# Block 0's attention logits: summed over features through DRAM and VectorE instead of on TensorE

## The chip, the core and the metric

The kernel runs on one core of one Trainium2 chip. The metric is the device time of one execution in microseconds (us), the median of several runs; lower is better. A core has engines that run side by side and wait for each other by semaphores: TensorE (matrix products, called PE in the profile; PEld is its loading of weights), VectorE (DVE), ScalarE (ACT), GpSimd (POOL) and SyncE (SP), which here only issues transfers. 16 DMA engines move data between DRAM and the on-chip memory SBUF. TensorE writes to PSUM, eight banks here, from which VectorE and ScalarE read.

## The reference

Two layers alternate, each twice, on x of 2048 tokens by 1024 features in bfloat16. Every layer normalises x over its features, computes a sum to add to x, and adds it.

```python
# layer A, on the normalised x; H = 32 heads of Dh = 32, W = 8 positions at a distance of 2
qkv = (x @ wqkv).reshape(B, S, 3, H, Dh).transpose(2, 0, 3, 1, 4)
q, k, v = qkv[0], qkv[1], qkv[2]
idx = pos[:, None] - (jnp.arange(W) * 2)[None, :]
logits = jnp.einsum("bhsd,bhswd->bhsw", q, kg) * Dh ** -0.5     # kg, vg: k, v at idx
logits = jnp.where(idx >= 0, logits, -1e9)
o = jnp.einsum("bhsw,bhswd->bhsd", softmax(logits), vg)
return o.transpose(0, 2, 1, 3).reshape(B, S, D) @ wo
# layer B, on the normalised x; F = 3584
return (relu(x @ W_gate) * (x @ W_up)) @ W_down
# x = x + A(x); x = x + B(x); x = x + A(x); x = x + B(x)
```

So each token attends to itself and to seven earlier tokens, 2 to 14 positions back. A logit is the sum, over the 32 features of a head, of q times k.

## The kernel before

The tokens are cut into four blocks of 512, each block into four token tiles of 128. The four layers are numbered L = 0 to 3. TensorE's work is laid out in one sequence by hand: the q, k and v products of blocks 0 to 3 in layer 0 (`plan_proj`), with the output product of block 0 (`plan_wo`, called through `wo`) put between two groups of block 3; then for each block the gate and up products of layer 1 (`plan_gu`), an output product, and the down products (`plan_down`), and so on. A group is eight matmuls of 128x512 into one PSUM bank.

All instructions are given to a planner, `Plan`, with an estimated time. `on_pe` adds matmuls and advances a clock at 0.216 us each (`MM`). `at(t, f)` puts a step at time t. `on_dve` and `chain` hold VectorE's work: the chain is done in order, each link once its input is due, and the `on_dve` pieces go in between at their times. `slab` loads 1 MB of weights into the next free slot of a ring of five. In the end all steps are sorted by time and recorded in that order, so the times only decide the order in which the instructions stand in each engine's queue; on the chip every engine goes through its queue in order and waits where an input is missing. The plan's time 0 is some 7 to 11 us after the start of the profiled span.

Layer 0's block 0 is special (`first_logits`). For the other blocks q, k and v go through DRAM, and come back with a partition for each pair of token tile and head, where VectorE multiplies and sums over features within a partition (`mul`, `add3`, `fold` in `plan_attn`). For block 0 the columns of q and k are taken so that chunk c of eight holds, on partition p, feature 8p + c: four neighbouring partitions hold a head's 32 features, eight in each. They stay in SBUF. As each k chunk c arrives, VectorE multiplies it by q for all eight positions (`mul(c)`, 128x4096) and adds the product to two f32 sums, one for each half of the positions (`add(c, h)`, `lacc`). Chunk 7 is not added. The sums are split into bfloat16 terms: ScalarE casts (`split`), VectorE subtracts the cast (`rest`), twice, giving three terms; with the last product these are four 128x4096 operands. TensorE then sums the four partitions of each head by multiplying with the 0/1 matrix `wide` (`red`, 32 matmuls into two banks, four groups of columns each), ScalarE copies the result to SBUF (`out`), and the softmax (`soft_a`, `expo`, `soft_b`) starts. `red` stands in TensorE's sequence behind the first v group of the second half of block 1 (`step`, hooked at `("v", 1, 0)`).

After the softmax VectorE multiplies with v and sums over the positions (`pv_mul`, `pv_add`, eight pieces); each piece is stored to `o_d`, and SyncE reloads it transposed, in four pieces (`load_o`, the tile `oT`), for the output product. That is hooked behind step `("k", 0, 2)` of block 3. The output product is added to x, and `plan_ln` normalises x for layer 1; a transposing transfer of SyncE (`turn`, the tile `xnT`) brings it to the layout that the gate product needs.

In the start, SyncE issues, in this order: x of block 0, half of v's weights, q's weights, x of block 1, k's weights (into two ring slots), v's other half (`wv_0_1`), x of block 2; then the transposes of block 1's normalised x, the output weights, and x of block 3. `late_ln` normalises the blocks 1 to 3 at given times.

Of the kernel before, what the change touches and what calls it, by code (L numbers as in the profile page):

```python
# [9 lines left out]
BF16 = mybir.dt.bfloat16  # L10
# [6 lines left out]
H = 32  # L17
# [106 lines left out]
def kernel(  # L124
# [42 lines left out]
    neg_half = const.tile([P, TPB], F32, name="neg_half")  # L167
    zpad = const.tile([P, KC, HALO], BF16, name="zpad")
    maskc = const.tile([32, W, HALO], F32, name="maskc")
    wide = const.tile([P, H], BF16, name="wide")  # L170
    ring = wring.tile([P, 8 * RING, SLAB], BF16, name="ring")
    q_d = [dram.tile([D, BLK], BF16, name=f"q_d{b}") for b in range(NB)]
    k_d = [dram.tile([D, ROW], BF16, name=f"k_d{b}") for b in range(NB)]
    v_d = [dram.tile([D, ROW], BF16, name=f"v_d{b}") for b in range(NB)]
    o_d = [dram.tile([TPB, H, DH, P], BF16, name=f"o_d{b}") for b in range(NB)]
    x_blk = [xpool.tile([P, TPB, D], BF16, name=f"xb{b}") if b else None for b in range(NB)]
    x_tiles = [x_blk[t // TPB][:, t % TPB, :] if t >= TPB else xpool.tile([P, D], BF16, name=f"x{t}") for t in range(NT)]
# [5 lines left out]
        nc.gpsimd.memset(neg_half[:], -0.5)  # L183

    def consts_late():
        nc.gpsimd.memset(wide[:], 1.0)
        nc.gpsimd.affine_select(out=wide[:], in_=wide[:], pattern=[[-FG, H]], compare_op=ALU.is_ge,
                                fill=0.0, base=0, channel_multiplier=1)
        nc.gpsimd.affine_select(out=wide[:], in_=wide[:], pattern=[[FG, H]], compare_op=ALU.is_ge,
                                fill=0.0, base=FG - 1, channel_multiplier=-1)  # L190
        nc.gpsimd.memset(zpad[:], 0.0)
        for t in (v_d, k_d):
            nc.gpsimd.dma_start(_dram(t[0], 0, [[ROW, P], [P * ROW, KC], [1, HALO]]), zpad[:])
        nc.gpsimd.memset(maskc[:], 0.0)
        for w in range(1, W):
            nc.gpsimd.memset(maskc[:, w, 0:DIL * w], NEG)

    def slab(src_ap, name, start=-10.0):
        shp = list(src_ap.shape)

        def load():
            s["t"] = ring[:, 8 * s["slot"]:8 * s["slot"] + shp[1], 0:shp[2]]
            nc.sync.dma_start(s["t"], src_ap)

        s = plan.slab(load, start)
        return s
# [251 lines left out]

    def first_logits(st, tm):
        hold = {}
        terms = []

        def begin():
            hold["q"] = hm_pool.tile([P, KC, BLK], BF16, tag="q", name="q_fm")
            hold["k"] = hm_pool.tile([P, KC, HALO + BLK], BF16, tag="k", name="k_fm")
            nc.gpsimd.memset(hold["k"][:, :, 0:HALO], 0.0)

        def evict(nm, c, acc, t):
            def f():
                if nm == "q":
                    nc.scalar.copy(hold["q"][:, c, :], acc()[:])
                    return
                kt = hold["k"]
# [24 lines left out]
        def add(c, h):  # L501
            def f():
                if c == 1:
                    hold[("acc", h)] = tpose.tile([P, W // 2, BLK], F32, tag="T", name=f"lacc{h}")
                acc, ws = hold[("acc", h)], slice(4 * h, 4 * h + 4)
                nc.vector.tensor_tensor(acc[:], hold[("pr", 0)][:, ws] if c == 1 else acc[:], hold[("pr", c)][:, ws], op=ALU.add)
            return f

        def split(n, h):

            def f():
                if h == 0:
                    terms.append(at_pool.tile([P, W, BLK], BF16, tag="pr", name="term_0", bufs=2) if n == 0 else
                                 hm_pool.tile([P, W, BLK], BF16, tag="k", name="term_1"))
                nc.scalar.copy(terms[n][:, 4 * h:4 * h + 4], hold[("acc", h)][:])

            def after(now):
                t = max(now + 0.2, tm.get(("split", n, 0), 0.0))
                plan.at(t, f)
                tm[("split", n, h)] = t + 2.4  # L520
            return after

        def rest(n, h):
            def f():
                acc = hold[("acc", h)]
                if n == 1 and h == 0:
                    terms.append(hm_pool.tile([P, W, BLK], BF16, tag="q", name="term_2"))
                nc.vector.tensor_tensor(acc[:] if n == 0 else terms[2][:, 4 * h:4 * h + 4], acc[:],
                                        terms[n][:, 4 * h:4 * h + 4], op=ALU.subtract)
            return f  # L530

        def red():
            Ls = hold["L"] = [psum.tile([P, 4, P], F32, tag="acc", name=f"L{wh}") for wh in range(2)]
            for n, term in enumerate([hold[("pr", KC - 1)]] + terms):
                for wh in range(2):
                    for tq in range(TPB):
                        nc.tensor.matmul(Ls[wh][32 * tq:32 * tq + 32, :, :], lhsT=wide[:],  # L537
                                         rhs=term[:, 4 * wh:4 * wh + 4, tq * P:(tq + 1) * P],
                                         start=(n == 0), stop=(n == 3), skip_group_check=True, tile_position=(0, 32 * tq))

        def out():
            st["L"] = at_pool.tile([P, W, P], F32, tag="L", name="L_0_0")
            for wh in range(2):
                nc.scalar.copy(st["L"][:, 4 * wh:4 * wh + 4, :], hold["L"][wh][:])

        def step():
            e = plan.on_pe(9.5, red)
            plan.at(e + T_EV, out)
            tm["logits_in"] = e + T_EV + 1.5

        return {"evict": evict}, {("v", 1, 0): step}


    def plan_attn(L, b, ends, st, tm):
# [121 lines left out]
            plan.at(t + 0.2, expo)  # L676
            tm["exp"] = t + 2.2

        plan.chain.append(((lambda: tm["logits_in"]) if first else now, 3.0, soft_a, after_a))
        plan.chain.append((lambda: tm["exp"], 4.0, soft_b, None))  # L680

        def after_pv(t):
# [128 lines left out]
    wo_start = []  # L811
    attn = {}
    glu = {}
    later_hooks = []
    wo_hook = {("k", 0, 2): lambda: wo(0, 0)}

    def proj(L, b):
        st, tm = {}, {}
        if L == 0 and b == 0:
            hooks, later_hooks[:] = (lambda h: (h[0], [h[1]]))(first_logits(st, tm))  # L820
        else:
            hooks = later_hooks.pop() if later_hooks else wo_hook if L == 0 and b == NB - 1 else {}
        attn[(L, b)] = plan_attn(L, b, plan_proj(L, b, hooks), st, tm)

    def wo(L, b):
# [99 lines left out]
```

## Time and profile before

| what | value |
|---|---|
| median of 3 runs | 1621.34 us (1621.14 to 1622.3) |
| the profiled execution | 1621.7 us, its span 1620.0 us |
| TensorE busy | 1609.8 us, 99% of the span |
| VectorE, ScalarE, GpSimd busy | 1060.6, 450.5 and 111.1 us |
| granted TensorE clock, mean | 1.00 |
| q, k and v products of block 0 and 1 end at | 53.8 and 97.2 us |
| softmax of block 0 starts at | 93.04 us |
| output product of block 0 | 150.75 to 164.7 us |
| first gate product of layer 1 | 193.91 us |

The span is from the first to the last profiled instruction; the time of an execution is a little longer. A line of the timeline names start, length, engine, line of the kernel, operation, output and inputs, and how many instructions are merged (x4); in square brackets stands the idle time before it and what ended that. Matmuls overlap: a single one is shown with some 0.38 us, and they start 0.216 apart. The chain of waits is followed back from the last instruction to whatever released each step. "Landing" is the time from the issue of a transfer until its data are in place.

### The profile page before, as it was taken

The page shows a single profiled execution, that of the slowest core. Times are in us where ns is not written, and L with a number is a line of the kernel's source. Part 1 is how long each engine was busy: PE and PEld are TensorE (multiplying, and loading weights), DVE is VectorE, ACT ScalarE, POOL GpSimd, SP SyncE. Part 2 cuts the span into 40 slices and gives each one's busy share as a digit, 9 for nine tenths or more (in the row PEclk, how much of TensorE's full clock was granted, in tenths as well). Part 3 has the DMA queues.
Part 4 walks back from the last instruction along what each step waited for, and adds up shares of the span by engine and source line. Part 5 has one row for each costly group of instructions (what it writes and reads, how often), then busy time and mean ns, then how long its engine had stood idle before and what let it go on. Part 6 is the DMA issues. An engine that isn't in the chain of part 4 may idle for free.

```text
span 1620.0 us, 19174 instructions
## 1 busy us (share of the span) xinstructions
PE 1609.8 (99%) x7609; PEld 745.5 (46%) x7658; DVE 1060.6 (65%) x1284; ACT 450.5 (28%) x707; POOL 111.1 (7%) x172
## 2 busy tenths in 40 slices
PE   8999999999999999999999999999999999999999
PEld 6444444444444444444444444444444444444444
DVE  6999989989999269960699617986989212211211
ACT  4753421304131241312413251133011311221110
POOL 3221000001010100011000110000000000000000
PEclk9999999999999999999999999999999999999999
DMA  9765878868965887668876699599846655564452
GB/s 299 162 157 136 222 197 219 189 190 216 223 181 196 231 206 206 189 204 234 198 202 195 212 240 209 159 281 225 228 155 194 184 169 163 175 186 152 156 167 68
DMA packets 443755, 314.83 MB, mean 194 GB/s; under 512 B 195568, under 2 KB 437648, under 8 KB 443664
## 3 DMA queue, kind: packets, MB, share of 16 engines
q1 hardware_dynamic: 414496, 281.39, 64.7%
q10 hardware_dynamic: 24368, 23.40, 4.4%
q0 software_dynamic: 4800, 8.80, 1.6%
q8 instruction: 60, 0.98, 0.3%
q14 instruction: 31, 0.25, 0.0%
HBM read 261.77 MB, written 36.05 MB: 184 GB/s over the span
## 4 chain that ended last, share of the span: by engine, by line
PE 98%; DMA 1%; SPq 1%; issue 0%; DVE 0%; DVEq 0%
PE acc_u L736 24%; PE acc_g L736 24%; PE dacc L782 24%; PE acc_k L401 7%; PE acc_wo L706 7%; PE acc_v L401 6%; PE acc_q L401 6%; DMA ring<-in_A_wqkv_dram 1%; SPq L850 0%; PE L L537 0%; SPq L834 0%; SPq L861 0%; DVE xb L790 0%; SPq L854 0%; SPq L838 0%
## 5 line engine op out<-in xcount | busy, mean ns | idle before, releaser
L736 PEld LDWEIGHTS <-ring 128*128 128x128 bf16 x3584 | 350.7, 98 | 422.9
L736 PE MATMUL acc_g<-xnT,ring 128*128 128x512 bf16 x1792 | 423.3, 379 | 0.0
L736 PE MATMUL acc_u<-xnT,ring 128*128 128x512 bf16 x1792 | 423.3, 379 | 0.0
L782 PE MATMUL dacc<-ring,hT 128*128 128x512 bf16 (+1 forms) x1787 | 386.4, 376 | 1.7
L751 DVE TENSOR_TENSOR hT<-acc_u,r 128x512 bf16<-128x512 f32 x224 | 154.3, 689 | 322.3 <-PE acc_u L736 316.7
L743 ACT ACTIVATE r<-acc_g 128x512 bf16<-128x512 f32 x224 | 133.6, 596 | 706.4 <-PE acc_g L736 706.4
L782 PEld LDWEIGHTS <-hT 128*128 128x128 bf16 x1820 | 178.1, 98 | 209.0
L401 PEld LDWEIGHTS <-ring 128*128 128x128 bf16 x1152 | 115.5, 100 | 134.0 <-DMA ring<-in_A_wqkv_dram 1.0
L627 DVE TENSOR_TENSOR pvt<-a,vhm 128x4096 bf16<-128x4096 bf16 x64 | 146.2, 2284 | 0.2
L586 DVE TENSOR_TENSOR l<-l,pr 128x1024 f32<-128x1024 f32 x112 | 136.8, 1221 | 2.3
L576 DVE TENSOR_TENSOR pr<-qhm,khm 128x4096 bf16<-128x4096 bf16 x56 | 127.9, 2283 | 13.1 <-DMA khm<-k_d 13.1
L401 PE MATMUL acc_k<-xnT,ring 128*128 128x512 bf16 x512 | 113.5, 379 | 0.6 <-DMA ring<-in_A_wqkv_dram 0.6
L706 PE MATMUL acc_wo<-ring,oT 128*128 128x512 bf16 x496 | 111.0, 379 | 0.8
L790 DVE TENSOR_TENSOR xb<-dacc,xb 128x512 bf16<-128x512 f32 (+1 forms) x49 | 32.6, 678 | 120.4 <-PE dacc L782 120.0
L401 PE MATMUL acc_v<-xnT,ring 128*128 128x512 bf16 x384 | 84.4, 379 | 0.0
L635 DVE TENSOR_TENSOR pvt<-pvt 128x2048 bf16<-128x2048 bf16 x64 | 78.1, 1221 | 1.3
L638 POOL DMA_DIRECT2D o_d<-ohm x64 | 35.3, 552 | 623.4 <-DVE ohm L637 612.6
L706 PEld LDWEIGHTS <-oT 128*128 128x128 bf16 x512 | 50.1, 98 | 60.4
L410 ACT CAST stage_q<-acc_q 128x512 bf16<-128x512 f32 x56 | 32.2, 583 | 148.7 <-PE acc_q L401 147.8
L586 DVE TENSOR_TENSOR l<-pr 128x1024 f32<-128x1024 bf16 x56 | 68.2, 1218 | 0.6
L593 DVE TENSOR_TENSOR l<-l 128x512 f32<-128x512 f32 x112 | 62.3, 556 | 3.0
L261 POOL TENSOR_TENSOR rstd<-vpe,neg_half 128x2 f32<-128x2 f32 x26 | 26.7, 1026 | 540.8 <-DVE vpe L260 540.6
(92 smaller groups left out, 844.9 us busy)
## 6 DMA issues: line engine op xcount, KB each, us to landing
ring<-in_B_W_gate_dram SPq DMA_DIRECT2D x56, 1024.0 KB, 7.0
ring<-in_B_W_up_dram SPq DMA_DIRECT2D x56, 1024.0 KB, 5.5
ring<-in_B_W_down_dram SPq DMA_DIRECT2D x48, 1024.0 KB, 6.1
ring<-in_A_wqkv_dram SPq DMA_DIRECT2D x27, 1024.0 KB, 5.4
ring<-in_A_wo_dram SPq DMA_DIRECT2D x16, 1024.0 KB, 7.0
vhm<-v_d SPq DMA_DIRECT2D x32, 284.0 KB, 7.0
v_d<-stage_v ACTq DMA_DIRECT2D x32, 256.0 KB, 6.0
o_d<-ohm POOLq DMA_DIRECT2D x64, 128.0 KB, 3.9
```

The lines of the kernel that those rows point to most:

```text
L401: nc.tensor.matmul(acc[:, t0 * P:t1 * P], lhsT=lhsT, rhs=xnT[(L, b)][:, t0:t1, kc, :], start=(kc == 0), stop=(kc == KC - 1))
L576: nc.vector.tensor_tensor(pr[:], st["q"][:], _ap(st["k"], HALO - DIL * w, [[HALO + P, DH], [1, P]]), op=ALU.mult)
L586: nc.vector.tensor_tensor(l[:], pr[:, 0:8] if i == 0 else l[:], pr[:, 8 * i + 8:8 * i + 16], op=ALU.add)
L593: nc.vector.tensor_tensor(l[:, 0:n], l[:, 0:n], l[:, n:2 * n], op=ALU.add)
L627: nc.vector.tensor_tensor(tt[:], a_bc, v_sh, op=ALU.mult)
L635: nc.vector.tensor_tensor(tt[:, 0:4], tt[:, 0:4], tt[:, 4:8], op=ALU.add)
L638: nc.gpsimd.dma_start(_dram(o_d[b], g * DG * P, [[DH * P, P], [1, DG * P]]), o[:].rearrange("p d t -> p (d t)"))
L706: nc.tensor.matmul(acc[:], lhsT=st["oT"][:, c, t, :], rhs=ws[half]["t"][:, c, :], start=(c == 0), stop=(c == KC - 1))
L736: nc.tensor.matmul(acc[:], lhsT=w["t"][:, kc, (j % 4) * P:(j % 4 + 1) * P], rhs=xnT[(L, b)][:, :, kc, :], start=(kc == 0), stop=(kc == KC ...
L743: nc.scalar.activation(r[:], hold.pop(("g", j))[:], ACT.Relu)
L751: nc.vector.tensor_tensor(st["hT"][:, j, :], hold.pop(("u", j))[:], hold.pop(("r", j))[:], op=ALU.mult)
L782: nc.tensor.matmul(accs[(t, c0)][:], lhsT=st["hT"][:, j, t * P:(t + 1) * P], rhs=w["t"][:, jl, c0 - half * SLAB:c0 - half * SLAB + n], sta ...
```

## The change

The sums of block 0 are made over all eight chunks, so the last product is added as well, and are kept in the order token tile, position, token (`lacc` is now `[P, TPB, W // 2, P]`). Each half (four positions) is stored to a new DRAM tile `l_d`, 1 MB of f32, by one SyncE transfer in rows of 2 KB, and loaded back by one more, 8 KB for each partition, so that a partition holds one pair of token tile and head, with the head's four partial sums side by side (`turn`). VectorE folds the four by two additions (`fold`: 128x1024, then 128x512). The casts, the subtractions, `wide`, the 32 matmuls and the copies out of PSUM are gone. The loaded halves take the buffers of block 0's q and k.

The output product of block 0 is hooked three groups later, behind `("q", 1, 1)` of block 3. v's other half is loaded later, in two transfers in place of one, x of block 2 later and in four transfers; the normalisation of block 3 has earlier times.

```diff
-    wide = const.tile([P, H], BF16, name="wide")
+    l_d = [dram.tile([TPB, P, W // 2, P], F32, name=f"l_d{h}") for h in range(2)]
...
-    def slab(src_ap, name, start=-10.0):
+    def slab(src_ap, name, start=-10.0, n=1):
...
-            nc.sync.dma_start(s["t"], src_ap)
+            for a in range(0, shp[1], shp[1] // n):
+                nc.sync.dma_start(s["t"][:, a:a + shp[1] // n], src_ap[:, a:a + shp[1] // n])
...
-                for h in range(2 if 0 < c < KC - 1 else 0):
-                    plan.chain.append((lambda: 0.0, 2.3, add(c, h), split(0, h) if c == KC - 2 else None))
-                if c == KC - 1:
-                    for n in range(2):
-                        for h in range(2):
-                            plan.chain.append((lambda n=n, h=h: tm[("split", n, h)], 2.3, rest(n, h),
-                                               split(1, h) if n == 0 else (lambda now: tm.__setitem__("logits", now))))
+                for h in range(2 if c else 0):
+                    plan.chain.append((lambda: 0.0, 2.3, add(c, h), turn(h) if c == KC - 1 else None))
+                for h in range(2 if c == KC - 1 else 0):
+                    plan.chain.append((lambda h=h: tm[("l_in", h)], 2.0, fold(h),
+                                       (lambda now: tm.__setitem__("logits", now)) if h else None))
...
+        def turn(h):
+
+            def store():
+                nc.sync.dma_start(l_d[h].rearrange("q p w t -> p q (w t)"),
+                                  hold[("acc", h)][:].rearrange("p q w t -> p q (w t)"))
+
+            def load():
+                hold[("l", h)] = hm_pool.tile([P, FG, W // 2, P], F32, tag="qk"[h], name=f"lhm{h}")
+                nc.sync.dma_start(hold[("l", h)][:].rearrange("p a w t -> p (a w t)"),
+                                  l_d[h].rearrange("q (h a) w t -> (q h) (a w t)", a=FG))
+
+            def after(now):
+                plan.at(now + 0.1, store)
+                plan.at(now + 2.5, load)
+                tm[("l_in", h)] = now + 11.0
+            return after
+
+        def fold(h):
+            def f():
...
+                l = hold[("l", h)]
+                nc.vector.tensor_tensor(l[:, 0:2], l[:, 0:2], l[:, 2:4], op=ALU.add)
+                nc.vector.tensor_tensor(st["L"][:, 4 * h:4 * h + 4, :], l[:, 0], l[:, 1], op=ALU.add)
+            return f
...
-        def red():
...
-    wo_hook = {("k", 0, 2): lambda: wo(0, 0)}
+    wo_hook = {("q", 1, 1): lambda: wo(0, 0)}
...
-    w0[("v", 1)] = slab(wqkv_v[:, :, 2 * D + SLAB:3 * D], "wv_0_1", -3.0)
+    w0[("v", 1)] = slab(wqkv_v[:, :, 2 * D + SLAB:3 * D], "wv_0_1", 19.9, 2)
...
-    for b, n, at in ((1, 4, -5.7), (2, 4, -2.5), (3, 2, 45.0)):
+    for b, n, at in ((1, 4, -5.7), (2, 1, 25.5), (3, 2, 45.0)):
...
-            late_ln(0, 3, 75.5, on_vector=True, norm_at=87.0)
+            late_ln(0, 3, 70.0, on_vector=True, norm_at=78.0)
```

In the order in which the built instructions stand, SyncE now issues, after the first transpose of block 1, the two transfers of v's other half, the second transpose, the four of block 2's x, the output weights and block 3's x. Later come the two stores and the two loads of the sums, behind them the two transposes of block 3, then q and k of block 1, the reload of block 0's attention output, v of block 1, and the first gate and up weights; the two transposes for the gate product stand behind the first and the second pair of these weights, where before both stood behind the first.

More of the change, by code (lines that the diff above doesn't have):

```diff
@@ L185, in consts_late @@
     def consts_late():
[L186 to L190, printed above, removed]
         nc.gpsimd.memset(zpad[:], 0.0)
@@ L463, in first_logits @@
         hold = {}
-        terms = []
         def begin():
@@ L503, in f @@
                 if c == 1:
-                    hold[("acc", h)] = tpose.tile([P, W // 2, BLK], F32, tag="T", name=f"lacc{h}")
-                acc, ws = hold[("acc", h)], slice(4 * h, 4 * h + 4)
-                nc.vector.tensor_tensor(acc[:], hold[("pr", 0)][:, ws] if c == 1 else acc[:], hold[("pr", c)][:, ws], op=ALU.add)
-            return f
-        def split(n, h):
+                    hold[("acc", h)] = tpose.tile([P, TPB, W // 2, P], F32, tag="T", name=f"lacc{h}")
+                acc = hold[("acc", h)][:].rearrange("p q w t -> p w q t")
@@ new lines, in f @@
+                first, more = (hold[("pr", i)][:, 4 * h:4 * h + 4].rearrange("p w (q t) -> p w q t", q=TPB) for i in (0, c))
+                nc.vector.tensor_tensor(acc, first if c == 1 else acc, more, op=ALU.add)
+            return f
+        def turn(h):
[11 more added lines that the diff above has]
+            return after
@@ L511, in f @@
+        def fold(h):
             def f():
                 if h == 0:
[L513 to L529, printed above, removed]
-            return f
-        def red():
[L533 to L551, printed above, removed]
+                    st["L"] = at_pool.tile([P, W, P], F32, tag="L", name="L_0_0")
+                l = hold[("l", h)]
@@ L554, in plan_attn @@
+                nc.vector.tensor_tensor(l[:, 0:2], l[:, 0:2], l[:, 2:4], op=ALU.add)
+                nc.vector.tensor_tensor(st["L"][:, 4 * h:4 * h + 4, :], l[:, 0], l[:, 1], op=ALU.add)
+            return f
+        return {"evict": evict}
     def plan_attn(L, b, ends, st, tm):
@@ L677, in after_a @@
             tm["exp"] = t + 2.2
-        plan.chain.append(((lambda: tm["logits_in"]) if first else now, 3.0, soft_a, after_a))
+        plan.chain.append((now, 3.0, soft_a, after_a))
         plan.chain.append((lambda: tm["exp"], 4.0, soft_b, None))
@@ L813 @@
     glu = {}
-    later_hooks = []
-    wo_hook = {("k", 0, 2): lambda: wo(0, 0)}
+    wo_hook = {("q", 1, 1): lambda: wo(0, 0)}
     def proj(L, b):
@@ L819, in proj @@
         if L == 0 and b == 0:
-            hooks, later_hooks[:] = (lambda h: (h[0], [h[1]]))(first_logits(st, tm))
+            hooks = first_logits(st, tm)
         else:
-            hooks = later_hooks.pop() if later_hooks else wo_hook if L == 0 and b == NB - 1 else {}
+            hooks = wo_hook if L == 0 and b == NB - 1 else {}
         attn[(L, b)] = plan_attn(L, b, plan_proj(L, b, hooks), st, tm)
```

## The prediction

> **What bounds the kernel now.** I read the page first (busy shares, chain of waits), then the chain in order of time, then the timelines of TensorE, VectorE and SyncE over the first 200 us. Times below are us from the start of the span, in the profile of before.
>
> The chain of waits, and three pieces of it in order of time (start, length, what):
>
> ```profile
> PE 98%; DMA 1%; SPq 1%; issue 0%; DVE 0%; DVEq 0%
> ...
> 9.98 16.99 DMA ring<-in_A_wqkv_dram
> ...
> 81.62 8.63 PE acc_v L401 x40
> 92.10 5.29 PE acc_v L401 x24
> ```
>
> TensorE is the path from 27 us to the end; the only hole in it is between 90.25 and 92.10. Before 27 us it is the second half of k's weights. TensorE's timeline (start, length, line, last the wait):
>
> ```profile
> 25.43 1.03 PE L401 MATMUL acc_k<-xnT,ring 128*128 128x512 bf16 x4
> 27.01 6.26 PE L401 MATMUL acc_k<-xnT,ring 128*128 128x512 bf16 x28 [0.56 <-DMA ring<-in_A_wqkv_dram]
> 33.11 7.07 PE L401 MATMUL acc_q<-xnT,wqv 128*128 128x512 bf16 x32
> ...
> 88.37 1.89 PE L401 MATMUL acc_v<-xnT,ring 128*128 128x512 bf16 x8
> 90.19 0.61 PE L537 MATMUL L<-prod,wide 128*32 128x512 bf16 x8
> 90.63 1.47 PE L537 MATMUL L<-term,wide 128*32 128x512 bf16 x24
> 92.03 5.35 PE L401 MATMUL acc_v<-xnT,ring 128*128 128x512 bf16 x24
> ...
> 150.75 13.98 PE L706 MATMUL acc_wo<-ring,oT 128*128 128x512 bf16 x62
> ```
>
> Starts give the pace: 32 matmuls every 6.91, so 0.216 each. From 27 us every group starts where the one before lets it, except at 90. So a change can gain what stands in the two holes, and lose whatever new hole it makes. VectorE, whose order decides the new holes:
>
> ```profile
> 78.34 4.49 DVE L528 TENSOR_TENSOR lacc<-lacc,term 128x2048 f32<-128x2048 f32 x2
> 82.74 4.54 DVE L528 TENSOR_TENSOR term<-lacc,term 128x2048 bf16<-128x2048 f32 x2
> 87.20 2.46 DVE L228 BATCH_NORM_STATS2 bst<-xb 128x6 f32<-128x512 bf16 x4
> ...
> 93.04 0.26 DVE L601 TENSOR_TENSOR L<-L,maskc 32x112 f32<-32x112 f32 x1
> ```
>
> Last, SyncE issues the reloads of block 0's attention output at 141.03; they landed in 3.9 to 5.4 us, so by 146.4 at the latest:
>
> ```profile
> 141.03 3.61 SPq L646 DMA_DIRECT2D oT<-o_d  x4
> ```
>
> **What the change does on TensorE.** (1) The 32 summing matmuls go. The eight v matmuls that start at 88.37 would be followed at 88.37 + 8 x 0.216 = 90.10; the next v matmul starts at 92.03. That is 1.93 us (1.84 if counted from the first sum at 90.19). I take 1.93.
>
> (2) v's rest (1 MB) and block 2 of x (1 MB) no longer go out right behind k. The k groups from 25.43 to 33.11 take 7.68 for 6.91 of work: 0.77 lost to k. The gain is between 0 and 0.77. For a gain: k's two halves landed 14.8 and 17.0 us after issue, v's rest shared the engines meanwhile. Against: it was queued behind k. I take 0.4, about the middle. The Trainium skill, "DMA: Bandwidth & Descriptors", section "Queues, rings and completion order", has it that each DMA engine consumes one queue's descriptors in ring order; by that rule alone a later transfer of the same queue can't hold k up, this term is 0 and the time is 1619.4 in place of 1619.0.
>
> (3) v's rest now follows the first transpose of block 1, which SyncE issues at 29.88 in 1.54. It goes out from 31.5, and its users start at 46.93. A 1 MB load landed in 5.4 to 7.0 by the page's medians, 17.5 at worst behind three other megabytes: 38 to 49. Cost 0 to 2; I take 0, since only one transpose is ahead of it.
>
> (4) The output product of block 0 moves behind three more groups of eight: 24 x 0.216 = 5.18 later, nothing on TensorE itself.
>
> Sum: -1.93 - 0.4 = -2.3. The span goes from 1620.0 to 1617.7, the profiled execution from 1621.7 to 1619.4; it lay 0.36 over the median of 1621.34, so the median becomes **1619.0**.
>
> **What lies beside it, and what covers it.** ScalarE loses four 128x2048 casts (1.90 each) and two copies; GpSimd three instructions of `wide` (0.14 + 2.07 + 2.15). Neither ends a wait of TensorE. On VectorE four instructions from 78.34 to 87.20 become two adds (4.49). The adds now write rows of 128; L627 (rows of 128) takes 2284 ns for 4096 elements and L576 2283, L496 in rows of 512 2.29 us, so the shape costs nothing.
>
> The trip through DRAM: with k 0.4 earlier the halves' sums end at 80.2 and 82.4. Block 3's statistics, due earlier now (70 for 75.5, still behind the adds in the built order), then fill VectorE (87.20 to 92.94, so 5.7) and wait for the last rstd, about 1.0: to 89.2. A 1 MB store is not in the trace. Stores in quiet stretches landed in 1.6 (64 KB), 1.7 (128 KB), 2.6 (256 KB). Low end: 1 MB at the 389 GB/s of the best slice, 2.7, and 1.4 for the rest: 4.1. High end: 0.9 more per 128 KB, 8.0. I take 6 for a store and 6 for a load (between the medians 5.4 and 7.0). Stores land at 86.3 and, sharing, 89.5; loads at 92.4 and 95.5; each half is then folded by 1.22 + 0.69 (rows 128x1024 and 128x512 f32), so softmax starts at 97.4 where it was 93.04: 4.4 later. Low end: 89.2 + 3.8 = 93.0, nothing later. High end, stores one after the other (88.3, 96.3), load 7, fold 1.9: 105.2, so 12.2 later.
>
> Attention output of block 0 shifts by as much. TensorE now comes for it at 150.75 - 2.3 + 5.2 = 153.6; the first piece landed by 146.4, so **7.2 us may be lost** before TensorE waits. 4.4 is covered with 2.8 left; without the move in (4) it would cost 2.
>
> SyncE's queue is in order. Behind the store that waits for VectorE stand the two transposes of block 3, which can't go before block 1's last matmul frees their buffer (97.2 - 2.3 = 94.9) and are used at 138.66 - 2.3, and block 1's q and k, used by VectorE after 138.26 + 4.4. Both have over 15 us. ScalarE's exponential waits with block 2's evictions behind it; eight accumulators of 1.73 cover 13.8. Block 2 of x is issued around 36 to 40 and lands in 11.3 to 17.0 by its own rows; ScalarE wants it at 47.61. Some us late there hold evictions, again under 13.8: nothing.
>
> After the output product come its normalisation and first gate matmul (193.91 - 2.3 = 191.6). The second transpose now stands behind two ring loads that need k's slots: free at 180.10 - 2.3 = 177.8, two issues 1.5, then the slowest landing of any transpose, 9.5: 188.8. Left: 2.8. Block 1's output product (290.64): the last reload stands behind a ring load at 289.07 - 2.3, takes 1.8 to issue and at most 8.2 to land: 296.8, wanted at 290.64 - 2.3 + 6 x 1.73 = 298.7. Both cost nothing, with little to spare.
>
> **Rivals.** (a) *The trip decides:* softmax of block 0 starts over 7.2 us later and the output product waits for its reload. Up to 9.5 the change still gains; from there it is slower than before. At the high end, 12.2: wait 5.0, so -2.3 + 5.0 = +2.7, 1624.0; over 1624.6 needs 12.8. For it: no 1 MB store in the trace, and SyncE alone issues all four transfers. Against: the DMA engines were 29% busy from 80 to 90, and issuing is short (the 1 MB x load of like rows at 6.01 took 1.09 of SyncE). The Trainium skill, "TensorE: Matmul & The Clock Gate", Part 1, says that an idle window of some 3.4 us halves the clock; the trace has no such hole after the start (granted clock 1.00 throughout). By that rule, as an estimate, a wait of 5 would cost some 1.7 more, 1625.7. (b) *A wait elsewhere:* v's rest late by up to 2, or one of the two reserves of 2.8 and 1.9 overdrawn by as much again. For it: SyncE's order changes through block 3 and the first gate stage. Against: each was figured with the slowest landing seen. -2.3 + 2 to + 5.6: 1621 to 1624.6. (c) *The k wait doesn't move:* the change does not do there what its words say; 1619.4. (d) *k's wait goes whole* and the runs fall on the low side: 1618.6, less 0.5 as the runs before scatter: 1618.1.
>
> **How the numbers follow.** 0.2% is 3.2 us, about what a measurement of this kernel tells from no change: faster means under 1618.1, slower over 1624.6. Forecast with (c) and the milder part of (d), 1618.2 to 1619.8: 0.56. (d) beyond 1618.1: 0.14. (a): 0.18, of which 0.10 over 1624.6, where several costs add. (b): 0.12, of which 0.08. So faster 0.14, slower 0.18, same 0.68. The range leaves out the far ends of (d) and of (a) and (b): 1617.8 to 1624.0; the forecast's own is 1618.2 to 1619.8.
>
> **What would show it.** v matmuls without a hole at 90: (1). acc_k in one group of 32: (2) whole. No wait at acc_v around 46, at acc_wo around 153, at acc_g around 191: the covers hold. Softmax's first instruction near 97 sizes the trip. A hole of over 5 us at acc_wo or acc_g, or a second hole later, would make the prediction wrong.

## The result, and the profile after

| | before | after |
|---|---|---|
| median, us | 1621.12 (1620.39 to 1622.30, 6 runs) | 1628.89 (1626.20 to 1630.11, 6 runs) |
| ratio | | 1.0047 [1.0034, 1.0060] |
| profiled execution, its span | 1621.7, 1620.0 | 1628.73, 1627.0 |
| first gate product of layer 1 | 193.91 | 198.75 |
| TensorE's own arrival there (the v group before it, start plus 32 x 0.216) | 193.9 | 191.35 |
| softmax of block 0 starts | 93.04 | 99.10 |

The kernel became slower by 7.8 us; 1619.0 was forecast, 1624.0 was the top of the range. The chain of waits by engine, and the group of the gate matmuls in the list of groups (busy, mean ns | idle time before, its releaser), both from the page of after:

```profile
PE 89%; DVE 6%; DMA 2%; issue 1%; ACT 1%; POOL 0%; SPq 0%; ACTq 0%; DVEq 0%; POOLq 0%
...
L713 PE MATMUL acc_g<-xnT,ring 128*128 128x512 bf16 x1792 | 425.0, 380 | 7.2 <-DMA v_d<-stage_v 7.2
```

TensorE was 98% of the chain and is 89%: somewhere the chain leaves it. All of the idle time that 1792 gate matmuls found is one wait of 7.2. TensorE's timeline of after, at the places where the prediction looked for holes:

```profile
25.49 7.16 PE L397 MATMUL acc_k<-xnT,ring 128*128 128x512 bf16 x32
32.49 7.07 PE L397 MATMUL acc_q<-xnT,wqv 128*128 128x512 bf16 x32
...
87.74 7.07 PE L397 MATMUL acc_v<-xnT,ring 128*128 128x512 bf16 x32
...
149.90 3.62 PE L397 MATMUL acc_q<-xnT,wqv 128*128 128x512 bf16 x16
153.35 13.98 PE L683 MATMUL acc_wo<-ring,oT 128*128 128x512 bf16 x62
...
184.44 7.07 PE L397 MATMUL acc_v<-xnT,ring 128*128 128x512 bf16 x32
198.75 3.57 PE L713 MATMUL acc_g<-xnT,ring 128*128 128x512 bf16 x8 [7.24 <-DMA v_d<-stage_v]
...
204.39 1.89 PE L713 MATMUL acc_g<-xnT,ring 128*128 128x512 bf16 x8
```

Up to 191 us everything came as hoped: k's group is whole (7.00 from start to start for 6.91), the hole at 90 is gone, the output product begins at 153.35 without a wait. Then TensorE stands from 191.35 to 198.75, that is 7.40, and the next sixteen matmuls take 204.39 - 198.75 = 5.64 for 16 x 0.216 = 3.45. These 2.19 are clock, as three rows of the table by stretches of after show (stretch, length, busy time of PE, PEld, DVE, ACT, POOL with counts, granted clock, DMA share, GB/s):

```profile
195.00:200.00 5.00, 1.25 (x4) 0.46 (x5) 2.16 (x1) 0.00 (x0) 0.00 (x0) 0.64 1.05 291
200.00:202.00 2.00, 2.00 (x6) 0.74 (x5) 0.00 (x0) 0.00 (x0) 0.00 (x0) 0.50 0.06 21
...
204.00:206.00 2.00, 2.00 (x11) 0.94 (x10) 1.34 (x2) 0.00 (x0) 0.00 (x0) 1.00 0.00 0
```

Six matmuls show in 2 us at clock 0.50, eleven at 1.00. The account closes: 193.91 - 191.35 = 2.56 gained, 7.40 + 2.19 = 9.59 lost, 7.0 net, and the spans differ by 7.0. Nothing else was lost in the profiled execution.

The releaser named, a store of v to DRAM, is only the event that came last by the profile. SyncE's own queue says more; first before, then after (start, time to issue):

```profile
174.40 7.52 SPq L278 DMA_TRANSPOSE xnT<-xn_all  x2
182.01 0.79 SPq L203 DMA_DIRECT2D ring<-in_B_W_gate_dram  x1
182.93 0.61 SPq L203 DMA_DIRECT2D ring<-in_B_W_up_dram  x1
```

```profile
176.58 1.97 SPq L274 DMA_TRANSPOSE xnT<-xn_all  x1
178.65 1.48 SPq L199 DMA_DIRECT2D ring<-in_B_W_gate_dram  x1
183.60 0.37 SPq L199 DMA_DIRECT2D ring<-in_B_W_up_dram  x1
188.62 4.04 SPq L274 DMA_TRANSPOSE xnT<-xn_all  x1
```

The second transpose, whose data the first gate matmul reads, stood ahead of the two 1 MB loads and now stands behind them. It was issued at 188.62 and landed 10.0 later, at 198.6; TensorE went on at 198.75. Of its lateness, 3.4 was a wait of the up load (L199) and 4.6 a wait of the transpose itself (L274), both put down by the profile to a store of k (`k_d`), which ScalarE issues. From the table of SyncE's waits (what waited, for what: us in total, times, longest):

```profile
SPq L274 <- DMA k_d<-stage_k: 4.6, 1, 4.6
...
SPq L199 <- DMA k_d<-stage_k: 3.4, 1, 3.4
```

The trip through DRAM, on VectorE in after:

```profile
77.70 4.49 DVE L499 TENSOR_TENSOR lacc<-lacc,prod 128x2048 f32<-128x2048 f32 x2
...
93.11 1.23 DVE L524 TENSOR_TENSOR lhm<-lhm 128x1024 f32<-128x1024 f32 x1 [3.84 <-DMA lhm<-l_d]
94.38 0.69 DVE L525 TENSOR_TENSOR L<-lhm 128x512 f32<-128x512 f32 x1
97.12 1.23 DVE L524 TENSOR_TENSOR lhm<-lhm 128x1024 f32<-128x1024 f32 x1 [2.05 <-DMA lhm<-l_d]
...
99.10 0.27 DVE L578 TENSOR_TENSOR L<-L,maskc 32x112 f32<-32x112 f32 x1
```

The stores landed in 4.9 and 6.9, the loads in 8.2 and 7.8 (6 each was taken). Softmax starts 6.06 later than before; 4.4 was forecast.

### The profile page after: what moved, and what is told of

It is laid out like the page before. It is cut to its first block, busy times and chain, and to the rows that moved or that the text cites. A ratio compares the mean times of both kernels' runs of the same rounds, so it can differ in the third digit from the quotient of the medians.

```text
span 1627.0 us, 19118 instructions
## 1 busy us (share of the span) xinstructions
PE 1610.5 (99%) x7577; PEld 745.2 (46%) x7626; DVE 1059.3 (65%) x1286; ACT 441.7 (27%) x701; POOL 104.2 (6%) x169
## 4 chain that ended last, share of the span: by engine, by line
PE 89%; DVE 6%; DMA 2%; issue 1%; ACT 1%; POOL 0%; SPq 0%; ACTq 0%; DVEq 0%; POOLq 0%
PE acc_g L713 24%; PE acc_u L713 24%; PE dacc L759 24%; PE acc_wo L683 6%; PE acc_k L397 4%; PE acc_q L397 4%; PE acc_v L397 4%; DVE pvt L604 1%; DVE lacc L499 1%; DVE l L563 1%; DVE pvt L612 1%; DVE pr L553 1%; DMA v_d<-stage_v 0%; DMA lhm<-l_d 0%; DMA k_d<-stage_k 0%
## 5 line engine op out<-in xcount | busy, mean ns | idle before, releaser
L553 DVE TENSOR_TENSOR pr<-qhm,khm 128x4096 bf16<-128x4096 bf16 x56 | 127.9, 2284 | 14.7 <-DMA khm<-k_d 14.7
L406 ACT CAST stage_q<-acc_q 128x512 bf16<-128x512 f32 x56 | 32.3, 582 | 153.6 <-PE acc_q L397 147.5
L397 PEld LDWEIGHTS <-wqv 128*128 128x128 bf16 x480 | 44.8, 104 | 40.7 <-issue 1.4
```

The source lines that it names most:

```text
L397: nc.tensor.matmul(acc[:, t0 * P:t1 * P], lhsT=lhsT, rhs=xnT[(L, b)][:, t0:t1, kc, :], start=(kc == 0), stop=(kc == KC - 1))
L553: nc.vector.tensor_tensor(pr[:], st["q"][:], _ap(st["k"], HALO - DIL * w, [[HALO + P, DH], [1, P]]), op=ALU.mult)
```

## The experiments

Theory A: the order of SyncE's queue is the loss. The later place of the output product lets the planner record the second transpose (its time 168.67) after the two loads (167.19). Rivals: the trip's lateness reaches the normalisation through VectorE (B); the wait on k's stores is what makes it late, not the loads (A1 against A2: the loads themselves). Later runs size the rest. The kernel before was run beside them each time: 1621.06 beside the first four runs (e1 to e4), 1620.89 (e5 to e8), 1621.17 (e9 to e12) and 1620.81 (e13, e14).

**The second pair of loads behind the transpose** (after, one edit):

```diff
-                sl = {"g": slab(wg_v[:, :, c0:c0 + SLAB], f"wg_{L}_{b}_{j // 4}"),
-                      "u": slab(wu_v[:, :, c0:c0 + SLAB], f"wu_{L}_{b}_{j // 4}")}
+                s0 = plan.pe - 22.0 if (L, b, j) == (1, 0, 4) else -10.0
+                sl = {"g": slab(wg_v[:, :, c0:c0 + SLAB], f"wg_{L}_{b}_{j // 4}", s0),
+                      "u": slab(wu_v[:, :, c0:c0 + SLAB], f"wu_{L}_{b}_{j // 4}", s0)}
```

> The changed kernel; only the second pair of gate and up weight loads of layer 1's block 0 is put behind the second transpose in SyncE's queue (in the changed kernel it stands ahead of it). Theory A (queue): the whole loss is the hole in front of the first gate product, and it comes from the second transpose being issued at 188.6 behind those two loads, the second of which and the transpose itself each wait for a k store of ScalarE that shares their semaphore. Then the transpose goes out about when its input is there (near 181), lands by 188, the hole at acc_g (7.4 us) and the slow clock behind it (2.2 us) go: span near 1617.4, time near 1618.5. Theory B (late normalisation): VectorE is 6 us late from the trip through DRAM, so the normalised rows come too late whatever the queue holds; then a hole of some 5 us or more stays and the time is over 1624.

Measured: 1618.73 (1618.16 to 1619.55), ratio 0.9984 [0.9975, 0.9994]. SyncE, then TensorE, in this kernel:

```profile
177.02 6.51 SPq L274 DMA_TRANSPOSE xnT<-xn_all  x2
183.62 1.87 SPq L199 DMA_DIRECT2D ring<-in_B_W_gate_dram  x1
```

```profile
183.94 7.07 PE L397 MATMUL acc_v<-xnT,ring 128*128 128x512 bf16 x32
190.84 1.89 PE L713 MATMUL acc_g<-xnT,ring 128*128 128x512 bf16 x8
```

The transposes go out one after the other and land in 5.7 and 6.4; hole and slow clock are gone. Softmax starts at 99.56, as late as in after, so B falls. It beats both kernels by the middle of its runs; the interval says faster than before by 0.06 to 0.25%.

**The hook alone** (before, with nothing of the trip in it):

```diff
-    wo_hook = {("k", 0, 2): lambda: wo(0, 0)}
+    wo_hook = {("q", 1, 1): lambda: wo(0, 0)}
```

> The kernel before; only the output product of block 0 is hooked three groups later, as in the changed kernel. Logits, sums on TensorE, x and v loads as before, so VectorE isn't late. The second transpose stands behind the second pair of gate and up loads, as in the changed kernel. Theory A (queue): it is late again, a hole of 3 to 8 us at acc_g, time 1624 to 1631. Theory B (VectorE late by the trip): no hole, 1621.1.

Measured: 1627.42 (1625.77 to 1627.75), ratio 1.0035 [1.0022, 1.0048]. TensorE in this kernel:

```profile
186.29 7.07 PE L401 MATMUL acc_v<-xnT,ring 128*128 128x512 bf16 x32
197.03 3.57 PE L736 MATMUL acc_g<-xnT,ring 128*128 128x512 bf16 x8 [3.67 <-issue]
...
203.16 1.89 PE L736 MATMUL acc_g<-xnT,ring 128*128 128x512 bf16 x8
```

And its SyncE:

```profile
180.97 0.54 SPq L203 DMA_DIRECT2D ring<-in_B_W_gate_dram  x1
181.60 0.56 SPq L203 DMA_DIRECT2D ring<-in_B_W_up_dram  x1
182.28 9.29 SPq L278 DMA_TRANSPOSE xnT<-xn_all  x1
```

The one-line edit by itself makes a loss of 6.4: a hole of 3.84 by starts, and 2.68 of slow clock after it (6.13 for 3.45). Here the transpose is not kept from starting; it takes 9.29 to issue and 14.7 to land.

**The hook one group of eight earlier** (after, `("q", 1, 0)` in place of `("q", 1, 1)`):

> The changed kernel; the output product of block 0 is hooked one group earlier (two groups later than before in place of three). The normalisation is then planned 1.7 us earlier and the second transpose stands ahead of the second pair of gate and up loads. TensorE comes for the output product near 151.6; the first reloaded piece landed near 152 in the changed kernel. Theory A: a hole of 0 to 1 us at acc_wo, none at acc_g: 1618.5 to 1619.5. Theory B: the hole at acc_g shrinks by only 1.7 to 3: 1624 to 1626.

Measured: 1618.83 (1618.50 to 1619.33), ratio 0.9986 [0.9976, 0.9995]; both transposes at 177.27 in 5.57, no hole at the output product or the gate product. A shift of 1.73 us in the place of one product is worth 10 us, because it decides which of two planned times, 1.5 apart, comes first.

**k's last two stores through GpSimd instead of ScalarE** (after; this takes away the waits on `k_d` and leaves both loads ahead):

```diff
-                nc.scalar.dma_start(_dram(kv[b], f0 * ROW + HALO, [[ROW, P], [P * ROW, 2], [1, BLK]]), s[:])
+                eng = nc.gpsimd if (L, b, nm, g) == (0, NB - 1, "k", 1) else nc.scalar
+                eng.dma_start(_dram(kv[b], f0 * ROW + HALO, [[ROW, P], [P * ROW, 2], [1, BLK]]), s[:])
```

> The changed kernel, order of SyncE's queue as in it; only block 3's last two stores of k go out from GpSimd's queue in place of ScalarE's, so that the second up load and the second transpose no longer share a semaphore with them. Theory A1 (shared semaphore): the second transpose goes out near 181 in place of 188.6 and lands by 191, hole under 2 us: 1618.5 to 1621. Theory A2 (the order alone: two 1 MB loads ahead of it on the DMA engines): it goes out early but lands late, a hole of 3 us or more stays: over 1622.

Measured: 1626.06 (1625.61 to 1627.54), ratio 1.0032 [1.0020, 1.0044]. SyncE in this kernel:

```profile
178.34 1.04 SPq L199 DMA_DIRECT2D ring<-in_B_W_gate_dram  x1
179.49 0.58 SPq L199 DMA_DIRECT2D ring<-in_B_W_up_dram  x1
180.16 11.33 SPq L274 DMA_TRANSPOSE xnT<-xn_all  x1
```

TensorE in this kernel, and how long the two transposes took from issue to landing (the least is the first one's, the most the second one's):

```profile
183.92 7.07 PE L397 MATMUL acc_v<-xnT,ring 128*128 128x512 bf16 x32
196.38 3.57 PE L714 MATMUL acc_g<-xnT,ring 128*128 128x512 bf16 x8 [5.39 <-DMA xnT<-xn_all]
...
DMA to landing us min/median/max: 6.3/11.2/16.1
```

The waits on `k_d` are gone, so they came with k's stores from ScalarE; that the two share a semaphore, as the expectations have it, is a reading that the profile doesn't show. Without the waits the transpose starts 8.5 earlier and lands only 2.3 earlier (16.1 after its start, at 196.3). So the waits are worth 2 to 3 us of the loss, and A1 falls as the whole cause: with nothing to wait for, the transpose behind the loads is still late. Why 16.1, though? In the profile of before a transpose at 796.17, behind two 1 MB loads issued 2.9 and 1.2 earlier and one of 284 KB between them, landed in 9.5: the very row that the prediction used. Two differences were left, the loads being closer ahead, and the stores of k and v that two other engines issue here at the same time.

**Only the up load behind the transpose**, the gate load still ahead (the edit of the first experiment, on `"u"` alone):

> The kernel after with only the up load of block 0's second pair moved behind the second transpose; the gate load of 1 MB still stands ahead of it. Theory (each megabyte queued ahead makes the transpose later): the transpose goes out at about 180 and lands, half as late as in the kernel after, by about 190 to 194: a hole at acc_g of 0 to 3 and a time of 1618.7 to 1623. Rival (only the shared semaphore of the up load and k's store made it late): no hole at all, 1618.7. Rival (one load ahead costs as much as two): a hole of 5 to 7, 1626 to 1629.

Measured: 1621.12 (1619.88 to 1624.05), ratio 1.0002 [0.9993, 1.0011], 2.3 to 2.4 over the kernels with no load ahead, and inside the theory's 1618.7 to 1623. TensorE and SyncE in its profiled execution, which took 1619.88, the least of its runs:

```profile
184.13 7.07 PE L397 MATMUL acc_v<-xnT,ring 128*128 128x512 bf16 x32
192.09 1.89 PE L713 MATMUL acc_g<-xnT,ring 128*128 128x512 bf16 x8 [0.89 <-DMA xnT<-xn_all]
```

```profile
178.17 1.40 SPq L199 DMA_DIRECT2D ring<-in_B_W_gate_dram  x1
183.04 4.70 SPq L274 DMA_TRANSPOSE xnT<-xn_all  x1
187.84 0.53 SPq L199 DMA_DIRECT2D ring<-in_B_W_up_dram  x1
```

**The same with k's stores through GpSimd** (the edits of e4_k_gpsimd and e7_one_ahead together):

> e4_k_gpsimd with the up load behind the second transpose, the gate load alone ahead, and no wait on k's stores from ScalarE. Theory (each megabyte right ahead of the transpose adds to its landing): halfway between 6 and 16.1, so issued at 179.5 in about 6.5 and landed 11 later at 190.5: no hole or under 0.5 at acc_g, and 1618.7 to 1619.5. Rival (one load ahead does as much as two): landed 14 to 16 later, a hole of 3 to 5, 1624 to 1626.

Measured: 1623.04 (1620.86 to 1625.34), ratio 1.0013 [1.0004, 1.0023], 3.5 over the upper end expected and below the rival's 1624. TensorE in its profiled execution, which took 1621.77, 1.3 less than the middle of the runs:

```profile
184.44 7.07 PE L397 MATMUL acc_v<-xnT,ring 128*128 128x512 bf16 x32
193.83 1.90 PE L714 MATMUL acc_g<-xnT,ring 128*128 128x512 bf16 x8 [2.32 <-DMA xnT<-xn_all]
```

One load ahead is worse here than in e7_one_ahead by the middle of the runs, though no store holds the transpose back: it starts earlier (180.61), takes 6.06 to issue and 13.2 to land. By bytes ahead alone it would have been 11, so that theory misses; the rival's 14 to 16 is missed too. Whether it matters that k's stores go through GpSimd here was not separated.

**Both loads ahead, and no stores beside them** (e4_k_gpsimd without block 3's late stores in layer 0; block 2's go to both blocks instead):

```diff
-                eng = nc.gpsimd if (L, b, nm, g) == (0, NB - 1, "k", 1) else nc.scalar
-                eng.dma_start(_dram(kv[b], f0 * ROW + HALO, [[ROW, P], [P * ROW, 2], [1, BLK]]), s[:])
+                late = L == 0 and (nm, g) in (("k", 1), ("v", 0), ("v", 1))
+                for d in range(b, b + (2 if b == NB - 2 else 0 if b == NB - 1 else 1) if late else b + 1):
+                    nc.scalar.dma_start(_dram(kv[d], f0 * ROW + HALO, [[ROW, P], [P * ROW, 2], [1, BLK]]), s[:])
```

> e4_k_gpsimd without the stores of block 3's v and of the second half of its k in layer 0, which in e4_k_gpsimd go out from ScalarE and GpSimd at 177.6 to 192 while the transpose is under way, 256 KB each; block 2's are stored twice in their place, so block 3 attends to block 2's values there. Both loads are still ahead of the transpose in SyncE's queue. Theory (the two loads ahead are enough): the transpose still takes about 11 to issue and 16 to land from 180, hole at acc_g about 5, 1626. Rival (the stores of the other queues share the DMA engines, and make the 9.5 that such a transpose took at 796 in the kernel before into 16): 7.5 to issue, 9.5 to land, there by 190, no hole, 1618.7 to 1619.5. In between, the share of each can be read from the landing.

Measured: 1618.58 (1618.24 to 1619.28), ratio 0.9987 [0.9977, 0.9996]. SyncE, then TensorE, in this kernel:

```profile
178.97 0.94 SPq L199 DMA_DIRECT2D ring<-in_B_W_gate_dram  x1
180.02 0.58 SPq L199 DMA_DIRECT2D ring<-in_B_W_up_dram  x1
180.70 8.42 SPq L274 DMA_TRANSPOSE xnT<-xn_all  x1
...
DMA to landing us min/median/max: 4.4/7.4/10.4
```

```profile
184.12 7.07 PE L397 MATMUL acc_v<-xnT,ring 128*128 128x512 bf16 x32
191.23 1.89 PE L715 MATMUL acc_g<-xnT,ring 128*128 128x512 bf16 x8
```

SyncE's queue goes as in e4_k_gpsimd to within 0.7 us up to the transpose; this takes 8.42 to issue and 10.4 to land, and the gate product waits 0.2. So the hole takes two things: the loads ahead, and the stores beside. The first transpose of this kernel, with neither, landed in 4.4. The loads alone make that 10.4, near the 9.5 of the row. With the stores alone the second transpose landed in 6.2 to 7.8 (before, e1_order, e3_hook_q10, e5_hook_k03, e8_hook_and_order, e11_order_again). Together they make 14.7 and 16.1, more than the two added.

The table puts the profiled executions in a row, one for each kernel, with the second transpose. Hole: the gate product's start less the arrival. Slow: its first sixteen matmuls over 3.45.

| kernel | loads ahead | stores beside | starts | to issue | to land | hole | slow |
|---|---|---|---|---|---|---|---|
| e1_order | 0 | yes | 181.3 | 2.3 | 6.4 | 0 | 0 |
| e13_no_late_stores | 2 | no | 180.70 | 8.42 | 10.4 | 0.2 | 0 |
| e14_k_gpsimd_one_ahead | 1 | yes | 180.61 | 6.06 | 13.2 | 2.5 | 0 |
| e2_hook_alone | 2 | yes | 182.28 | 9.29 | 14.7 | 3.84 | 2.68 |
| e4_k_gpsimd | 2 | yes | 180.16 | 11.33 | 16.1 | 5.55 | 1.88 |
| e7_one_ahead | 1 | yes | 183.04 | 4.70 | 8.9 | 1.05 | 0 |
| after | 2 | yes | 188.62 | 4.04 | 10.0 | 7.40 | 2.19 |

In the last two the transpose was kept from starting by 3.4 and 8.0 us of waits on k's stores, during which part of the loads went by; that may be why its landing is shorter. The Trainium skill, "DMA: Bandwidth & Descriptors", section "Queues, rings and completion order", says that a DMA engine works through one queue in the order of its ring. That fits the first half (behind two loads 10.4, behind none 4.4); it doesn't price the second, what other queues take meanwhile.

**Before with the hook and the loads in order** (the edits of e2_hook_alone and e1_order together):

> The kernel before with two edits: block 0's output product three groups later, as in e2_hook_alone, and the gate and up loads behind the second transpose. Nothing of the trip through DRAM is in it. Theory (the loss comes from the queue order alone): no hole at acc_g, the two transposes one after the other at about 175 to 183, and the time of the kernel before, 1621.1 (1620.5 to 1621.8). Rival (the later output product costs something else too): 1622 to 1627.

Measured: 1621.48 (1620.42 to 1622.18), ratio 1.0003 [0.9994, 1.0012]; no hole at the gate product, both transposes at 177.88 in 6.04. With e2_hook_alone this settles it: the same hook costs 6.4 with the loads ahead (1627.42 against 1621.06) and 0.6, not told from nothing, with them behind.

**Was the move of the product needed?** After, with the hook two groups earlier, at `("k", 0, 3)`, so that the order is right by itself and TensorE comes early for the output product:

> The kernel after, with block 0's output product two groups of eight earlier (in k's last group instead of q's, one group later than before), so that the second transpose is ahead of the gate and up loads again by the planner's own count. Theory (the loss is the order of SyncE's queue): no hole at acc_g; both transposes issued as one pair at about 175 to 183. At acc_wo TensorE now comes at about 149.4, and the first piece of the attention output, issued at 147.1 and landing in 4.2 to 5.1, is there at 151.5 to 152: a hole of 2.1 to 2.6 there, so 1618.7 + 2.3 = 1621.0; if a hole that short costs clock as well, up to 2 more, 1623. Rival (the later place of the output product is what costs, by anything other than the queue): part of the hole at acc_g stays. Rival (the trip's lateness is covered here too): no hole at acc_wo, 1618.7.

Measured: 1620.51 (1620.28 to 1620.71), ratio 0.9997 [0.9988, 1.0005]. TensorE in this kernel:

```profile
151.14 13.99 PE L683 MATMUL acc_wo<-ring,oT 128*128 128x512 bf16 x64 [1.31 <-DMA oT<-o_d]
```

The trip's lateness shows: a wait of 1.31 on the attention output (1.47 by starts), and 1620.51 - 1618.8 = 1.7 over the kernels without it, a little under what was expected. The hole is short, and the clock stays at 1.00. The product one group earlier still, where it stood before, would wait some 1.47 + 1.73 = 3.2 (an estimate; no run has it, since by the planner's times its first matmul would be recorded ahead of the last reload there). By this estimate a later place was needed; this late was not.

**What the early loads cost k** (e1_order, with v's rest and block 2 of x sent as early and in as large pieces as before):

```diff
-    w0[("v", 1)] = slab(wqkv_v[:, :, 2 * D + SLAB:3 * D], "wv_0_1", 19.9, 2)
+    w0[("v", 1)] = slab(wqkv_v[:, :, 2 * D + SLAB:3 * D], "wv_0_1", -3.0)
-    for b, n, at in ((1, 4, -5.7), (2, 1, 25.5), (3, 2, 45.0)):
+    for b, n, at in ((1, 4, -5.7), (2, 4, -2.5), (3, 2, 45.0)):
```

> The kernel e1_order (the kernel after, with the gate and up loads behind the second transpose) with v's rest and block 2 of x loaded as early and in as large pieces as in the kernel before. Theory (they took the engines' time from k's second half): acc_k is again split in two with a wait of about 0.6, first group to q 7.6 instead of 7.0, so 0.6 to 0.8 longer than e1_order: 1619.3 to 1619.5. Rival (a later transfer of the same queue can't hold k up): acc_k in one group, 1618.7.

Measured: 1620.31 (1619.11 to 1621.24), yet its profiled execution, 1619.34, had no wait for k. Inconclusive: the middle of the runs spoke for one theory, the trace for the other, and the companion had run on another chip. So four kernels went together on one chip:

> e1_order once more, as the companion on the same chip for the three kernels below: 1618.7 (1618.2 to 1619.6), and in its profile acc_k as one group and q's second group beginning between 32.0 and 32.5.

> e6_loads_back once more, beside e1_order on one chip, since e6_loads_back took 1620.3 in the middle of its runs and only 1619.3 in the profiled one, which showed no wait for k. Theory (v's rest and block 2 of x, sent early, hold k's second half up by an amount that changes from run to run, 0 to 2): again 1619 to 1621.3, 1.0 to 1.7 longer than e1_order in the middle, with a spread two or three times as wide. Rival (the two jobs differed by the chip): no longer than e1_order by more than 0.4, which is what the profiled starts of q's second group say on average (32.67 in four profiles with the early loads, 32.26 in six with the late ones).

> e1_order with only v's rest loaded as early as in the kernel before, right behind k's second half; block 2 of x stays late. If the megabyte next to k in the queue is what holds k up: 1619.7 to 1620.4, as e6_loads_back. If it is x or the two together: 1618.7 to 1619.2.

> e1_order with only block 2 of x loaded early, in one transfer as in the kernel before, now right behind k's second half; v's rest stays late. If any megabyte behind k holds it up: 1619.7 to 1620.4. If only v's rest does, or only the two together: 1618.7 to 1619.2.

| kernel | early | median, us | ratio to before |
|---|---|---|---|
| e11_order_again | neither | 1618.87 (1618.23 to 1620.11) | 0.9986 [0.9977, 0.9995] |
| e9_v_early | v's rest | 1619.21 (1618.73 to 1619.86) | 0.9987 [0.9978, 0.9996] |
| e10_x_early | x | 1619.30 (1618.70 to 1619.96) | 0.9987 [0.9978, 0.9996] |
| e12_loads_back_again | both | 1619.98 (1618.98 to 1620.74) | 0.9992 [0.9983, 1.0001] |

Both together cost 1.11, one alone 0.3 to 0.4, which by runs that scatter over 1.1 to 1.9 is not told from nothing. The spread that was expected to be two or three times as wide was not: 1.76 against 1.88. TensorE with both early this time shows the wait:

```profile
24.92 1.03 PE L397 MATMUL acc_k<-xnT,ring 128*128 128x512 bf16 x4
26.97 6.26 PE L397 MATMUL acc_k<-xnT,ring 128*128 128x512 bf16 x28 [1.02 <-DMA ring<-in_A_wqkv_dram]
33.07 7.07 PE L397 MATMUL acc_q<-xnT,wqv 128*128 128x512 bf16 x32
```

From start to start k takes 8.15 for 6.91, so 1.24 lost; e6_loads_back lost none. Part of the 1.24 is that k begins early in this execution (24.92, against 25.50 in e11_order_again): q's second group begins 0.66 later than there (33.07 against 32.41). Of the five profiled kernels that load both early (before, e2_hook_alone, e6_loads_back, e8_hook_and_order, e12_loads_back_again) two waited for k and three did not; of the nine that load both late (after and eight made from it) none did. The wait differs from one execution to the next, so one profile can't size it.

## Why the prediction was wrong

**The step that failed** is the last reserve of the prediction: "The second transpose now stands behind two ring loads that need k's slots: free at 180.10 - 2.3 = 177.8, two issues 1.5, then the slowest landing of any transpose, 9.5: 188.8. Left: 2.8." The new order was seen and the arrival of TensorE was right (191.6 forecast, 191.35 measured). The landing was not. 9.5 is the row at 796 in the profile of before, a transpose behind loads and with no store of another queue beside it; e13_no_late_stores, which makes the place nearly that, lands in 10.4, at 191.1, and takes no harm. But at 180 ScalarE is storing block 3's k and v. With these beside it, the transpose took 14.7 and 16.1 (e2_hook_alone, e4_k_gpsimd); and in after the queue itself stood still on the same stores, 3.4 before the up load and 4.6 before the transpose, which started at 188.62 and not at 179.3. Either way it landed at 196.3 to 198.6, not 188.8. The hole of over 5 us at acc_g, which the prediction named as a sign of being wrong, came. The bound was the slowest row of the trace, but of a place with other neighbours.

**The bound was too near.** The rival that held this place, a reserve overdrawn "by as much again", ended 5.6 over the forecast, at 1624.6 (a reserve of 2.8 overdrawn by as much again makes a hole of 2.8; the sum uses twice that). The hole alone is 7.4. It also left out the clock, 2.19 more, which the prediction had priced, from the Trainium skill, only for a wait at the output product. The Trainium skill, "TensorE: Matmul & The Clock Gate", Part 1, has an idle window of some 3.4 us halving the clock; these runs agree: after holes of 3.84, 5.55 and 7.40 the granted clock was 0.50, after 1.05, 1.47 and 2.5 it stayed 1.00. The price was 1.9 to 2.7.

**The sum came out, its split is open.** With the queue in order the change gives 1618.73 and 1618.87 against 1621.06 and 1621.17, so -2.3 in both jobs, as forecast. The traces bear out term (1), 1.93: from q's second group to the gate product, e6_loads_back takes 158.85 and e8_hook_and_order, with the sums still on TensorE, 160.80. They don't contradict term (2), k's wait, taken as 0.4 "about the middle" of 0 to 0.77: in the five profiled kernels with both loads early k lost 0.77, 1.24 and three times nothing, 0.40 in the mean, so the bound of 0.77 from one execution was too low and the middle was a lucky guess. The medians say otherwise. By them the early loads cost 1.11 in the kernel with its queue in order, and the rest of the change is worth 1621.17 - 1619.98 = 1.2 (0.6 in the other job). The intervals are wide enough for either split, so the -2.3 doesn't prove its terms. The 0 that the prediction drew from the Trainium skill's ring order fits neither: k did wait in two of the five (0.56 and 1.02), and in none with the loads late.

**What held:** v's rest landed in time (no wait at 46.30); the shape of the adds cost nothing (4.49 for two); fold took 1.23 + 0.69; the output product came without a wait at 153.35 (153.6 forecast), and block 1's likewise, since the wait of 7.2 is the only long one of TensorE in after. The trip was mis-sized by 1.7 (99.10 for 97.4): both transfers took longer than the 6 taken, at most 6.9 and 8.2. Rival (a), the trip deciding, did not come about in after; e5_hook_k03 shows it 3.5 us further up the sequence. One reading of before was loose: only the first reload of the attention output had landed by 146.4; the last was issued at 143.8.

## What to carry to other kernels

When work is moved in a kernel whose queues are sorted by planned times, list every transfer whose neighbours change, in its own queue and in the others at that time; the slowest landing of the trace is a bound only for a place with the same neighbours. A reserve of 2 to 3 us in front of TensorE is worth defending: a hole of 3.84 to 7.40 cost here 1.9 to 2.7 us of clock on top, and where two planned times decide it, the order is better written down (here by one start time). A wait that varies from run to run can't be sized by one profile: take medians on one chip beside it, and say so where the two don't agree.

## What the runs showed of the hardware

Issuing a transposing transfer took SyncE 2.0 us with no load ahead (after, the first one), 8.42 with 2 MB ahead and 9.29 and 11.33 with stores of other queues beside: the issuing engine is held up, and all that stands behind in its queue. 256 KB stores on the queues of ScalarE and GpSimd added 5.7 to the landing of a transpose on SyncE's that stood behind 2 MB (10.4 to 16.1, one execution each). A load of SyncE and a transpose waited for stores that ScalarE had issued (3.4 and 4.6); moving those stores to GpSimd took these waits away. And two megabytes queued behind k's weights made the kernel longer by 1.11 in the middle of the runs, although the same queue took them after k; TensorE waited for k in two of five profiled executions with them and in none of nine without. By what path they hold k up was not tried.
